# A new hand-written order of the 1,380 steps of a fused attention and mixture kernel on one core

## The chip, the cores and the metric

One core of one Trainium2 chip. The metric is device microseconds of one execution; lower is better. The time shown for a kernel is the median of several runs.

## What is computed

Eight batches of 512 tokens in 8 heads of 64, and 32 state rows a head. Both directions of a small cross attention are made, and their results go side by side through one wide layer with a "snake" activation:

```python
scores = scale * x @ state.T ;  a  = softmax(scores)  ;  xread = a @ state     # 512 rows a batch
scores2 = scale * state @ x.T;  a2 = softmax(scores2) ;  sread = a2 @ x        # 32 rows a batch
x = concat([xread, sread])            # 8 * 544 = 4352 rows of 512
h = x @ w_in                          # 512 -> 2048
g = h + sin(alpha * h)**2 / (alpha + 1e-9)
out = g @ w_out                       # 2048 -> 512
```

## The kernel before, in words

There is no loop. A list of names, `ORDER`, is written out by hand, and the kernel walks through it and calls one small function for each name. Each engine has a queue of its own and works through its instructions in the order in which the list issued them; the framework puts in the waits that the data and the buffers need. So the list fixes what stands ahead of what on TensorE (PE), VectorE (DVE), ScalarE (ACT), GpSimd (POOL) and the DMA queues of SyncE (SP) and POOL. Where a step's name ends in A, V or G it runs on ACT, DVE or POOL. A number after `t` below is the batch; "batch 8" is the 256 `sread` rows.

The steps, with the lines that the profile shows for them:

- `lq`, `l_s01` (SP queue, L261, L249), `l_st`, `li.s`, `lo.s`, `lx.b` (POOL queue, L267, L282, L294, L275): loads. `li.s` is the s-th quarter of w_in, `lo.s` the s-th quarter of w_out, 512 KB each as they arrive; `lx.b` is x of batch b. DMA steps of POOL stand in the same queue as its arithmetic.
- `warm_up.n.c.bank` (L303): n matmuls on zeros with c columns, whose result nobody reads.
- `st_t`, `st_c` (L333, L340): transpose of the state and copies out of PSUM; `xtq`, `xt`, `xc`, `at`, `ac` the same for x of batches 0 and 1 and for the weights of batch 0.
- `sc` (L399) scores, `ex` (L406) exponential, `rs`, `rr` (L410, L416) row sums and reciprocals, `nm` (L201, "A<-E,rR") normalising on POOL, `ad` (L440) a DMA transpose of the result for batches 1 to 7.
- `pk`, `td` (L348, L389): x of a batch repacked by DVE and transposed by DMA on the SP queue, which `sc` of that batch needs.
- `m.b.s` and `me` (L488, L496): state times a quarter (or two) of w_in, and its copies out of PSUM. h of the `xread` rows is then made from `m` directly, with the softmax weights as the moving operand. `m` uses the PE array in pieces of 64x32.
- `w`, `cs`, `rc`, `xs` (L450, L461, L468, L471): the `sread` side; `cs` uses the array in pieces of 128x64.
- `hg`, `h.t.f` (L552, L537, L543): h of batch t for the f-th 128 of 2048 columns; `si` (L560) sine, `sq` (L569 on ACT, L201 on DVE or POOL) its square, `gt` (L576) g.
- `o.t.st.f0.f1` (L587): out of 128 rows, from g of blocks f0 to f1-1; `oc`, `os` (L595, L602) copy and store.

Each matmul step names its PSUM bank (0 to 7); a bank can be written again only when the reader of its last content is through (for an `h`, that is its `gt`). The last sixteen matmuls, `oh.7.3.1`, fill a quarter of the columns of one row block.

```python
for step in ORDER:
    name, *args = step.split(".")
    getattr(steps, name)(*(int(a) if a.isdigit() else a for a in args))
```

Of the kernel before, what the change touches and what calls it, by code (L numbers as in the profile page):

```python
# [33 lines left out]
warm_up.2.128.2 gt.0.2 si.0.0 warm_up.2.128.2 warm_up.2.128.6 warm_up.2.128.3 warm_up.2.128.2
warm_up.2.128.6 me.0.1.0.A gt.0.1 sq.0.0.G m.0.2.3.2 si.0.3 m.1.2.5.6 hg.0.4.0.7 me.0.2.0.V
me.0.2.1.A hg.0.4.1 sq.0.3.G hg.0.6.0.4 me.1.2.1.V hg.0.6.1 si.0.4 hg.0.7.0.3 hg.0.11.0.2 me.1.2.0.V
si.0.6 hg.0.7.1 sq.0.4.G hg.0.5.0.6 gt.0.0 hg.0.5.1 si.0.7 hg.0.11.1 hg.0.8.0.5 hg.0.8.1 sq.0.6.A
gt.0.3 sq.0.7.G o.0.3.0.2.0 si.0.5 gt.0.4 o.0.3.2.3 o.0.0.0.2.1 si.0.11 o.0.0.2.3 gt.0.6 sq.0.5.G
o.0.0.3.4 o.0.2.0.1.7 si.0.8 o.0.3.3.5 sq.0.11.A gt.0.7 hg.0.9.0.4 sq.0.8.G o.0.2.1.2 gt.0.5
o.0.2.2.4 hg.0.9.1 gt.0.11 o.0.0.4.5 hg.0.10.0.3 si.0.9 o.0.2.4.5 gt.0.8 o.0.0.5.6 o.0.3.5.6  # L40
sq.0.9.A o.0.3.6.8 pk.1.0.V hg.0.10.1 xt.1.1.6 pk.1.1.V si.0.10 gt.0.9 xt.1.0.2 xc.1.1.0.A sq.0.10.G
o.0.2.5.6 xc.1.1.1.V xc.1.0.0.A o.0.0.6.7 xc.1.0.1.V o.0.0.7.8 o.0.2.6.7 sc.1.1.5 gt.0.10 sc.1.0.4
m.0.3.6.2 ex.1.0 o.0.2.7.8 me.0.3.0.V o.0.1.0.3.3 me.0.3.1.V o.0.1.3.6 hg.0.13.0.6 o.0.1.6.7 ex.1.1
rs.1.0 hg.0.13.1 m.1.3.2.4 si.0.13 o.0.1.7.8 rr.1.0 rs.1.1 nm.1.0.0.4.G o.0.1.8.9 hg.0.12.0.5
o.0.3.8.9 rr.1.1 hg.0.12.1 me.1.3.0.V o.0.0.8.9 nm.1.1.0.4.G o.0.1.9.10 o.0.0.9.10 me.1.3.1.V
si.0.12 o.0.0.10.11 o.0.3.9.11 sq.0.13.G ad.1 hg.0.15.0.2 sq.0.12.A o.0.1.10.12 hg.0.15.1 gt.0.12
o.0.2.8.10 si.0.15 o.0.2.10.11 gt.0.13 o.0.0.11.12 hg.0.14.0.4 sq.0.15.A hg.0.14.1 o.0.3.11.13
si.0.14 gt.0.15 o.0.0.12.13 o.0.1.12.13 o.0.3.13.14 sq.0.14.A pk.2.0.V o.0.1.13.14 pk.2.1.V h.1.2.5
gt.0.14 h.1.4.6 td.2 si.1.2 lx.3.0.1 h.1.0.2 si.1.4 o.0.0.13.15 sq.1.2.V h.1.1.4 si.1.0 gt.1.2
sq.1.4.G o.0.3.14.16 si.1.1 o.0.2.11.13 sq.1.0.A oc.0.3.V h.1.6.5 sq.1.1.G gt.1.4 o.0.2.13.14 os.0.3  # L50
h.1.3.0 si.1.6 gt.1.0 o.0.1.14.16 si.1.3 sq.1.6.G h.1.13.6 gt.1.1 oc.0.1.A o.0.2.14.15 o.0.0.15.16
si.1.13 h.1.15.2 sq.1.3.G gt.1.6 os.0.1 o.0.2.15.16 oc.0.0.A h.1.5.4 sq.1.13.G oc.0.2.V si.1.15
h.1.7.3 os.0.0 gt.1.3 o.1.1.0.1.5 si.1.5 os.0.2 h.1.8.1 sq.1.15.G gt.1.13 o.1.1.1.2 si.1.7
o.1.2.0.2.7 sq.1.5.A o.1.1.2.3 sq.1.7.G h.1.12.0 gt.1.15 si.1.8 h.1.9.6 gt.1.5 o.1.2.2.3 si.1.12
sq.1.8.G o.1.2.3.5 gt.1.7 si.1.9 o.1.1.3.4 h.1.10.2 sq.1.12.A pk.3.1.V h.1.11.4 sq.1.9.G gt.1.8
o.1.2.5.6 si.1.10 o.1.2.6.7 gt.1.12 h.1.14.3 si.1.11 sq.1.10.G o.1.2.7.8 gt.1.9 sc.2.1.1 si.1.14
o.1.1.4.7 sq.1.11.A pk.3.0.V sq.1.14.G o.1.1.7.8 gt.1.10 td.3 o.1.2.8.9 sc.2.0.0 o.1.1.8.9 gt.1.11
o.1.1.9.10 ex.2.0 o.1.3.0.2.6 gt.1.14 o.1.3.2.4 o.1.2.9.10 o.1.3.4.5 o.1.2.10.12 ex.2.1 o.1.2.12.13
rs.2.0 o.1.1.10.11 m.2.2.2.4.3.0 rr.2.0 rs.2.1 o.1.2.13.14 nm.2.0.0.4.G me.2.3.0.A o.1.2.14.15 w.0.1
rr.2.1 me.2.2.1.A me.2.3.1.V o.1.3.5.6 nm.2.1.0.4.G me.2.2.0.A o.1.3.6.7 o.1.2.15.16 cs.0 oc.1.2.A  # L60
m.2.0.3.4.0.2 ad.2 rc.0 o.1.3.7.8 me.2.1.1.A o.1.3.8.9 sc.3.0.7 xs.0.1 me.2.1.0.A o.1.1.11.12 os.1.2
me.2.0.0.V sc.3.1.2 me.2.0.1.A o.1.1.12.13 o.1.3.9.10 xs.0.0 o.1.3.10.11 ex.3.0 o.1.1.13.16 ex.3.1
rs.3.0 o.1.3.11.13 oc.1.1.A o.1.3.13.14 rr.3.0 h.2.0.0 rs.3.1 nm.3.0.0.4.G os.1.1 o.1.3.14.16 si.2.0
rr.3.1 h.2.1.3 oc.1.3.V nm.3.1.0.4.G h.2.2.4 h.2.8.1 os.1.3 h.2.3.7 lx.4.0.1 ad.3 si.2.2 o.1.0.0.3.2
si.2.8 sq.2.0.V o.1.0.3.4 sq.2.2.G gt.2.0 h.2.4.5 si.2.1 o.1.0.4.6 si.2.3 sq.2.8.G o.1.0.6.7 gt.2.2
h.2.9.6 si.2.4 o.2.3.0.1.0 o.1.0.7.8 sq.2.1.G o.1.0.8.9 sq.2.3.A gt.2.8 o.1.0.9.10 h.2.5.4 si.2.9
gt.2.3 o.1.0.10.11 sq.2.4.G o.1.0.11.12 si.2.5 h.2.7.1 gt.2.1 o.1.0.12.13 sq.2.9.A sq.2.5.G
o.1.0.13.14 gt.2.4 o.1.0.14.15 si.2.7 o.1.0.15.16 o.2.0.0.1.7 gt.2.9 o.2.0.1.2 oc.1.0.A h.2.6.3
sq.2.7.G gt.2.5 o.2.3.1.2 os.1.0 o.2.3.2.3 si.2.6 h.2.10.5 pk.4.1.V pk.4.0.V o.2.3.3.4 sq.2.6.A
# [594 lines left out]
```

## Time and profile before

| | |
|---|---|
| median of 7 runs | 221.22 us (221.15 to 221.54) |
| the profiled execution | 221.41 us, of which the span is 219.5 |
| TensorE clock granted | 1.00 |
| PE busy | 210.0 us (96%), 1593 matmul records |
| DVE, ACT, POOL busy | 162.2 (74%), 173.4 (79%), 107.0 (49%) |
| o (L587), h (L537) | 133.9 and 60.0 us busy |
| loads of w_in, w_out, x | 512 KB each, 10.9, 17.6, 7.5 us from issue to landing (medians) |

The span runs from the first to the last instruction; the 1.9 us around it are start and end of the program. A row of the timeline has the start, the time until the last of its instructions ended, the engine, the line and how many instructions it merges; idle time ahead of it and what ended that stand in brackets. Matmuls overlap: a matmul of 512 columns is shown with 0.38 us, but in a dense row one starts every 0.216 us.

### The profile page before, as it was taken

Reading aid. Unit: us, or ns where it says so; the run is one execution under the profiler, and the core shown is the slowest. Engines: PE = TensorE matmul, PEld = TensorE weight load, DVE = VectorE, ACT = ScalarE, POOL = GpSimd, SP = SyncE. Lnnn points to the kernel's source line nnn. Section 1 sums busy time; section 2 is a strip of 40 time slices with the busy share of each in tenths; the row PEclk is TensorE's granted clock in tenths of the full one; section 3 lists DMA queues with packets and bytes.
Section 4 is the critical chain, followed back from the end, with each engine's and each line's share of the span. In section 5 each row is a group of like instructions: output and inputs, shape, how many; then the busy total and the mean of one; then the engine's idle time right before and its main releaser. Section 6 shows DMA issues by size and latency. Waiting matters only on the chain.

```text
span 219.5 us, 4304 instructions
## 1 busy us (share of the span) xinstructions
PE 210.0 (96%) x1593; PEld 104.5 (48%) x1619; DVE 162.2 (74%) x286; ACT 173.4 (79%) x297; POOL 107.0 (49%) x115
## 2 busy tenths in 40 slices
PE   6789999999999999999999999999999999999994
PEld 3644544444444534444454444444444555665452
DVE  2769896999668889989888788888667987671201
ACT  4699878997899979898996999798858896685111
POOL 5959534795296647743943387273501082121000
PEclk9999999999999999999999999999999999999999
DMA  6999999935378529167135327470220211012042
GB/s 184 194 207 204 205 204 124 212 128 96 99 159 129 99 78 154 51 152 92 51 72 127 114 77 96 130 114 0 48 100 0 99 48 48 0 51 96 1 143 96
DMA packets 38052, 23.48 MB, mean 107 GB/s; under 512 B 20992, under 2 KB 33680, under 8 KB 38032
## 3 DMA queue, kind: packets, MB, share of 16 engines
q1 hardware_dynamic: 26128, 15.08, 26.2%
q0 software_dynamic: 11648, 8.13, 26.0%
q8 instruction: 12, 0.20, 0.4%
q14 instruction: 8, 0.07, 0.1%
q10 hardware_dynamic: 256, 0.01, 0.1%
HBM read 17.44 MB, written 8.91 MB: 120 GB/s over the span
## 4 chain that ended last, share of the span: by engine, by line
PE 86%; DMA 4%; ACT 3%; DVE 2%; POOL 2%; issue 1%
PE o_ps L587 51%; PE h_ps L537 20%; PE m_ps L488 4%; PE h_ps L543 3%; DMA st_nat<-in_state_dram 3%; PE h_ps L552 3%; DVE gT L576 2%; PE w_ps L450 2%; POOL s L201 2%; PE s_ps L399 1%; PE w_ps L461 1%; DMA s<-in_state_dram 1%; ACT s L560 1%; PE warm_ps L303 1%; ACT L226 1%
## 5 line engine op out<-in xcount | busy, mean ns | idle before, releaser
L587 PE MATMUL o_ps<-w_out_sb,gT 128*128 128x512 bf16 (+2 forms) x542 | 133.9, 373 | 1.6 <-issue 1.0
L576 DVE SCALAR_TENSOR_TENSOR gT<-s,inva_sb,h_ps 128x512 bf16<-128x512 bf16 (+1 forms) x144 | 96.6, 714 | 18.9 <-POOL s L201 9.7
L201 POOL TENSOR_TENSOR s<-s 128x512 bf16<-128x512 bf16 (+1 forms) x76 | 76.6, 1019 | 63.8 <-ACT s L560 61.7
L560 ACT ACTIVATE s<-h_ps,alpha_sb 128x512 bf16<-128x512 f32 (+1 forms) x144 | 88.7, 670 | 10.6 <-PE h_ps L543 4.5
L587 PEld LDWEIGHTS <-gT 128*128 128x128 bf16 x560 | 52.4, 98 | 60.3 <-issue 5.0
L537 PE MATMUL h_ps<-AT,M 128*128 128x512 bf16 x219 | 60.0, 379 | 0.3
L537 PEld LDWEIGHTS <-M 128*128 128x128 bf16 x224 | 21.8, 98 | 25.9 <-issue 0.4
L569 ACT ACTIVATE s<-s 128x512 bf16<-128x512 bf16 (+1 forms) x53 | 31.4, 594 | 0.8
L201 POOL TENSOR_TENSOR A<-E,rR 128x512 bf16<-128x512 bf16 x16 | 16.6, 1048 | 23.8 <-ACT o_sb L595 12.7
L595 ACT COPY o_sb<-o_ps 128x512 f32<-128x512 f32 (+2 forms) x24 | 13.7, 570 | 16.6 <-PE o_ps L587 16.5
L496 ACT CAST M<-m_ps 128x512 bf16<-128x512 f32 x35 | 18.6, 594 | 8.2 <-PE m_ps L488 8.2
L496 DVE CAST M<-m_ps 128x512 bf16<-128x512 f32 x29 | 18.9, 679 | 2.4 <-PE m_ps L488 2.1
L595 DVE COPY o_sb<-o_ps 128x512 f32<-128x512 f32 x11 | 7.6, 690 | 13.0 <-PE o_ps L587 12.9
L410 DVE TENSOR_REDUCE R<-E 128x16 f32<-128x512 bf16 x16 | 10.4, 658 | 1.2 <-ACT E L406 0.9
L201 DVE TENSOR_TENSOR s<-s 128x512 bf16<-128x512 bf16 (+1 forms) x15 | 6.2, 415 | 6.8 <-ACT s L560 6.7
L488 PE MATMUL m_ps<-w_in_sb,stT 64*32 64x512 bf16 x256 | 10.2, 382 | 0.0
L468 DVE RECIPROCAL rC<-w_ps 128x128 f32<-128x128 f32 x8 | 7.6, 948 | 3.3 <-PE w_ps L461 3.2
L552 PE MATMUL h_ps<-AT,M 128*128 128x512 bf16 x29 | 8.4, 379 | 1.0 <-ACT M L496 0.8
L303 PE MATMUL warm_ps<-warm 128*128 128x128 bf16 (+1 forms) x66 | 7.1, 260 | 2.2 <-DVE warm L209 2.0
L406 ACT ACTIVATE E<-s_ps 128x512 bf16<-128x512 f32 x16 | 8.9, 603 | 0.4 <-PE s_ps L399 0.3
L543 PE MATMUL h_ps<-xs_all,w_in_sb 128*128 128x256 bf16 x64 | 9.1, 273 | 0.0
L560 ACT ACT_TABLE_LOAD x5 | 6.4, 1283 | 2.2 <-PE h_ps L537 1.1
(56 smaller groups left out, 100.9 us busy)
## 6 DMA issues: line engine op xcount, KB each, us to landing
out_dram<-o_sb SPq DMA_DIRECT2D x33, 256.0 KB, 2.3
xnat<-in_x_dram POOLq DMA_DIRECT2D x7, 512.0 KB, 7.5
w_in_sb<-in_moe_w_in_dram POOLq DMA_DIRECT2D x4, 512.0 KB, 10.9
w_out_sb<-in_moe_w_out_dram POOLq DMA_DIRECT2D x4, 512.0 KB, 17.6
x<-in_x_dram SPq DMA_DIRECT2D x4, 256.0 KB, 4.1
st_nat<-in_state_dram POOLq DMA_DIRECT2D x1, 256.0 KB, 5.9
out_dram<-o_sb SPq DMA_DIRECT2D x1, 192.0 KB, 1.9
s<-in_state_dram SPq DMA_DIRECT2D x1, 128.0 KB, 2.3
```

Of the source, the lines that this page charges most:

```text
L201: {"V": k.nc.vector, "G": k.nc.gpsimd}[eng].tensor_tensor(out, a, b, ALU.mult)
L410: k.nc.vector.reduce_sum(R[:, g], k.t["E", b][:, g].rearrange("p c (h j) -> p (c h) j", j=k.Ns), axis=AX.X)
L488: k.nc.tensor.matmul(k.t["m", b, s + n, g][o0:o0 + k.Ns, :], k.stT[k.half(r), b * k.G + g, c0:c0 + k.Ns], k.w_in_sb[k.half(r), 2 * g + h, ...
L496: k.copy(eng)(k.t["M", b][:, g, s * k.FW:(s + 1) * k.FW], k.t["m", b, s, g][:])
L537: k.nc.tensor.matmul(hp[:, :n], k.t["M", t][:, g, fs], k.t["AT", t][:, g, :], start=(g == 0), stop=(g == k.G - 1),)
L543: k.nc.tensor.matmul(hp[:, :n], k.w_in_sb[:, q, fs], k.xs_all[:, q].rearrange("p b j -> p (b j)"), start=(q == 0), stop=(q == k.Q - 1),)
L552: k.nc.tensor.matmul(k.t["h", t, f][:], k.t["M", t][:, g, f * k.P:(f + 1) * k.P], k.t["AT", t][:, g, :], start=(g == 0), stop=(g == k.G - 1),)
L560: k.nc.scalar.activation(s[:, :n], k.t["h", t, f][:, :n], ACT.Sin, scale=k.alpha_sb[:, f:f + 1])
L569: k.nc.scalar.activation(s2[:, :n], s[:, :n], ACT.Square)
L576: k.nc.vector.scalar_tensor_tensor(gT[:, :n], k.t["s2", t, f][:, :n], k.inva_sb[:, f:f + 1], k.t["h", t, f][:, :n], ALU.mult, ALU.add,)
L587: k.nc.tensor.matmul(k.t["o", t, st, half][:, cols], k.t["gT", t, f][:, rows], k.w_out_sb[:, f, cols], start=(f == 0), stop=(f == k.FT - 1),)
L595: k.copy(eng)(o_sb[:, cols], k.t["o", t, st, half][:, cols])
```

## The change

Only `ORDER` changes: 1380 names become 1371. The steps that compute are the same (the matmuls in `o` are cut into 378 names and not 388), on the same lines; what differs is their order on the engines, the PSUM banks, and the engine of a few copies and squares: `sq` on ACT 53 to 48 and on POOL 76 to 81, `me` on ACT 35 to 36, `oc` on ACT 22 to 21, `st_c` on ACT 3 to 2, one `nm` from POOL to DVE. The warm-up matmuls go from 60 of 128 columns and 6 of 512 to 67 and 7. On POOL's queue `lx.1` and `lo.1` change places; `lo.0` stands behind `li.2` and ahead of `li.3` in both lists. The final steps stay the same, but `oc.7.2` moves from DVE to ACT.

The diff replaces the whole list. Its first part, and the stretches that the prediction speaks of:

```diff
-touch_x l_s01 zero.1 touch lq.0.S ident_ consts warm_up.2.128.0 warm_up.2.128.1 warm_up.2.128.2
-l_alpha lq.1.S zero.0 warm_up.6.512.3 exp_table lq.2.S identf.V lq.3.S s01_c.G l_st li.0 xq.0.A
-s01_t.4 li.1 xtq.0.5 xq.1.A s01_k.1.V s01_k.0.A li.2 xtq.1.6 xc.0.0.0.V xq.2.A xc.0.0.1.V lo.0
-al_t.7 xq.3.A xtq.2.0 al_c inva sc.0.0.1 lo.1 xc.0.1.0.A xtq.3.2 warm_up.2.128.3 ex.0.0
-warm_up.2.128.4 lx.1.0.1 warm_up.2.128.5 xc.0.1.1.V warm_up.2.128.6 warm_up.2.128.7 rs.0.0 sc.0.1.0
-li.3 st_t.0.3 ex.0.1 rr.0.0 st_t.1.4 lo.2 st_c.0.0.V st_c.0.1.A warm_up.2.128.5 warm_up.2.128.6
-warm_up.2.128.1 st_c.1.0.A rs.0.1 warm_up.2.128.2 warm_up.2.128.7 nm.0.0.0.4.G warm_up.2.128.0
-warm_up.2.128.5 st_c.1.1.A warm_up.2.128.3 warm_up.2.128.6 warm_up.2.128.1 rr.0.1 warm_up.2.128.2
-sin_table warm_up.2.128.7 warm_up.2.128.0 nm.0.1.0.4.G at.0.0.5 warm_up.2.128.3 ac.0.0.V m.0.0.6.4
...
-m.2.0.3.4.0.2 ad.2 rc.0 o.1.3.7.8 me.2.1.1.A o.1.3.8.9 sc.3.0.7 xs.0.1 me.2.1.0.A o.1.1.11.12 os.1.2
...
+touch_x l_s01 consts touch lq.0.S ident_ l_alpha lq.1.S zero.0 warm_up.7.512.3 exp_table lq.2.S
+zero.1 identf.V lq.3.S s01_c.G l_st li.0 xq.0.A xtq.0.4 warm_up.3.128.3 li.1 xq.1.A s01_t.5
+xc.0.0.0.V li.2 xtq.1.6 warm_up.5.128.3 xq.2.A s01_k.1.V lo.0 al_t.7 s01_k.0.A xc.0.0.1.V xtq.2.0
+warm_up.3.128.3 xq.3.A al_c sc.0.0.1 inva lx.1.0.1 xc.0.1.0.A xtq.3.2 warm_up.2.128.3
+warm_up.2.128.4 ex.0.0 lo.1 warm_up.2.128.5 xc.0.1.1.V warm_up.2.128.6 warm_up.2.128.7 sc.0.1.0
+rs.0.0 st_t.1.3 li.3 ex.0.1 st_t.0.4 rr.0.0 lo.2 st_c.1.1.A st_c.1.0.V warm_up.2.128.5
+warm_up.2.128.6 sin_table warm_up.2.128.2 rs.0.1 warm_up.2.128.7 warm_up.2.128.1 nm.0.0.0.4.G
+warm_up.2.128.0 warm_up.2.128.5 warm_up.2.128.3 warm_up.2.128.6 warm_up.2.128.2 rr.0.1
+warm_up.2.128.7 warm_up.2.128.1 st_c.0.0.V warm_up.2.128.0 warm_up.2.128.5 nm.0.1.0.4.G st_c.0.1.A
+at.0.0.3 warm_up.2.128.6 ac.0.0.V m.0.0.2.7 m.1.0.1.0 lo.3 at.0.1.5 me.0.0.1.A me.0.0.0.V
+warm_up.2.128.6 warm_up.2.128.4 me.1.0.1.A ac.0.1.V hg.0.2.0.3 me.1.0.0.V hg.0.0.0.7 hg.0.2.1
+hg.0.0.1 hg.0.3.0.6 si.0.2 lx.2.0.1 hg.0.3.1 m.1.1.2.4 si.0.0 m.0.1.5.0 hg.0.1.0.1 me.0.1.1.A
+sq.0.2.V hg.0.1.1 sq.0.0.G me.1.1.0.V me.1.1.1.A warm_up.2.128.0 gt.0.2 si.0.3 warm_up.2.128.0
+warm_up.2.128.2 warm_up.2.128.4 warm_up.2.128.0 warm_up.2.128.2 me.0.1.0.A gt.0.0 sq.0.3.G m.1.2.4.0
+si.0.1 m.0.2.3.2 hg.0.4.0.5 me.1.2.1.V me.0.2.0.A hg.0.4.1 sq.0.1.G hg.0.5.0.7 me.0.2.1.V hg.0.5.1
+si.0.4 hg.0.8.0.0 hg.0.10.0.3 me.1.2.0.V si.0.5 hg.0.10.1 sq.0.4.G hg.0.8.1 gt.0.1 hg.0.7.0.2
+si.0.10 o.0.2.0.1.4 hg.0.7.1 gt.0.3 si.0.8 sq.0.5.G o.0.2.1.3 hg.0.6.0.1 sq.0.10.A gt.0.4 o.0.2.3.4
...
+me.1.3.1.A o.0.0.14.15 o.0.3.13.14 pk.2.1.V me.1.3.0.A o.0.3.14.15 pk.2.0.V o.0.1.13.14 o.0.3.15.16
+o.0.1.14.15 td.2 h.1.2.2 oc.0.3.V h.1.1.1 si.1.2 lx.3.0.1 h.1.3.3 si.1.1 h.1.0.0 os.0.3 sq.1.2.V
...
+sc.2.0.0 si.1.5 gt.1.3 h.1.13.4 sq.1.4.G o.1.1.0.1.7 si.1.6 gt.1.14 o.1.1.1.2 h.1.8.3 sq.1.5.A
...
+me.2.0.1.V o.1.0.0.2.4 me.2.1.0.A o.1.2.9.10 me.2.0.0.V os.1.1 w.0.7 cs.0 sc.3.1.1 rc.0 sc.3.0.3
...
+gt.2.5 si.2.4 o.1.0.14.15 h.2.11.2 si.2.9 gt.2.2 h.2.10.1 sq.2.4.G o.1.0.15.16 si.2.11 gt.2.0
+h.2.7.6 sq.2.9.A sq.2.11.G gt.2.4 h.2.6.3 o.2.0.0.1.5 oc.1.0.A o.2.0.1.2 gt.2.9 o.2.0.2.3 si.2.6
+h.2.15.7 os.1.0 pk.4.1.V o.2.3.0.1.4 si.2.7 o.2.3.1.2 sq.2.6.G gt.2.11 o.2.3.2.4 si.2.10 o.2.3.4.6
+sq.2.7.A pk.4.0.V h.2.12.0 sq.2.10.G gt.2.6 td.4 h.2.13.2 si.2.15 gt.2.7 o.2.0.3.5 si.2.13 sq.2.15.G
...
```

Where the eight `cs` stand: before, `cs.0`, `cs.2`, `cs.3` and `cs.6` have an `m` right behind them, `cs.7` and `cs.5` stand together, `cs.1` and `cs.4` alone between full-array steps. After, `cs.2` has an `m` behind it and `cs.1` one ahead of it, `cs.7` and `cs.5` stand together, and `cs.0`, `cs.3`, `cs.4` and `cs.6` have neither.

## The prediction

> **What bounds the kernel now.** I read the page first, for the engine that is full, then the chain that ended last, the waits of PE, and the timeline of the stages where PE waits.
>
> ```profile
> PE 210.0 (96%) x1593; PEld 104.5 (48%) x1619; DVE 162.2 (74%) x286; ACT 173.4 (79%) x297; POOL 107.0 (49%) x115
> ...
> PE 86%; DMA 4%; ACT 3%; DVE 2%; POOL 2%; issue 1%
> ```
>
> PE is the bound, but 96% hides where its other time is. From the chain, piece by piece, and PE's own waits:
>
> ```profile
> 202.14 6.26 PE o_ps L587 x29
> ```
>
> ```profile
> PE x_ps L361 <- ACT xp L356: 1.0, 2, 0.8
> PE o_ps L587 <- issue: 1.0, 6, 0.2
> ```
>
> 29 matmuls in 6.26 us are 0.216 us each. PE waits only microseconds in all, and apart from the "issue" entry, which is mostly a matmul without a record behind an `m`, all of it is early. From 18.5 us to the end, I added 0.216 for each 512-column matmul, 0.109 for 256 columns, 0.029 for each of `sc` and `w`, and the blocks priced below: the sum follows the trace within 0.1 us to the last matmul. So after 18.5 us PE has nothing left to lose. An order can gain only before that, and lose anywhere.
>
> **Before 18.5 us.** These rows are ACT's chain:
>
> ```profile
> 10.59 1.45 ACT L340 COPY stT<-st_ps 64x384 bf16<-64x384 bf16 x3 [0.94 <-DVE stT L340]
> 12.06 1.28 ACT L226 ACT_TABLE_LOAD   x1
> ...
> 13.58 1.07 ACT L496 CAST M<-m_ps 128x512 bf16<-128x512 f32 x2
> 14.85 1.26 ACT L560 ACTIVATE s<-h_ps,alpha_sb 128x512 bf16<-128x512 f32 x2 [0.19 <-PE h_ps L552]
> ...
> 17.62 0.60 ACT L496 CAST M<-m_ps 128x512 bf16<-128x512 f32 x1
> ```
>
> The last copy ends at 18.22 and lets go the steady stage at 18.27. The loads set floors: the state lands at 9.28, the first three quarters of w_in at 11.8, 15.2 and 17.1 (issue times 4.16, 4.90 and 5.63, plus 7.7, 10.3 and 11.5 to landing). POOL's first ten issues are the same but for one swap, so these stay.
>
> The new list gives ACT one `st_c` less ahead of the sine table, so table and first copies of M come some 0.5 us earlier. Something else takes that wait's place. The bracket of the first row shows that the two engines' copies of one transposed block go one after the other, in the list's order; the new list puts ACT's first. DVE's `st_c.1.0.V` then starts at about 10.5 (10.0 + 0.47) instead of 10.0, and behind it in DVE's queue stand `rs.0.1`, `rr.0.1`, and then POOL's `nm.0.1`:
>
> ```profile
> 10.00 0.55 DVE L340 COPY stT<-st_ps 64x384 bf16<-64x384 bf16 x1 [0.26 <-PE st_ps L333]
> ...
> 11.58 1.05 POOL L201 TENSOR_TENSOR A<-E,rR 128x512 bf16<-128x512 bf16 x1 [0.19 <-DVE rR L416]
> ```
>
> So `nm.0.1` runs 12.1 to 13.15, `at.0.1` goes at 13.3, `ac.0.1` 13.75 to 14.2, and `hg.0.2.1` at 14.2, where it is now (14.22, behind ACT's copy). From there both lists hold the same chain with other block numbers: four `hg`, two `m`, six warm-ups, ACT's six instructions. **Nothing gained**; bounds -0.2 (the 0.5 comes through, until the quarter landing at 15.2 stops it) and +0.1. The seven added warm-up matmuls and the earlier `consts` lie in waits for loads; the two before `at.0.0` (2 x 0.056 = 0.11) end before `nm.0.1` does. Without that cover they cost 0.11.
>
> `lx.1` ahead of `lo.1`: each landing is about 2.6 us behind the one before (19.7, 22.2, 24.9 by the tiles' answers). x of batch 1 comes at 22.4 and is first used (`xt.1.1`) at 23.3; the second quarter of w_out comes at 24.9 and is first used (`o.0.0.4.5`) at 25.4, both placed by counting 0.216s from 18.27. Cost nothing, hidden by 0.9 and 0.5 us of matmuls; without that cover, the lateness itself.
>
> **Blocks in pieces of the array.** Here the new list costs something certain. `cs` alone, and `cs` with `m` behind it:
>
> ```profile
> 150.87 1.03 PE L537 MATMUL h_ps<-AT,M 128*128 128x512 bf16 x4
> 151.83 0.41 PE L461 MATMUL w_ps<-E,ones 128*64 128x128 bf16 x8
> 152.18 1.25 PE L587 MATMUL o_ps<-w_out_sb,gT 128*128 128x512 bf16 x5
> ```
>
> ```profile
> 163.85 0.63 PE L450 MATMUL w_ps<-E,xp 128*128 128x64 bf16 x16
> 164.41 0.41 PE L461 MATMUL w_ps<-E,ones 128*64 128x128 bf16 x8
> 164.76 0.62 PE L488 MATMUL m_ps<-w_in_sb,stT 64*32 64x512 bf16 x16
> 165.54 0.81 PE L587 MATMUL o_ps<-w_out_sb,gT 128*128 128x512 bf16 x3 [0.16 <-issue]
> ```
>
> Alone: 150.87 + 4 x 0.216 = 151.73 to 152.18 is 0.45. An `m` of 16 alone (78.19 to 78.85 in PE's timeline) is 0.66. Together: 163.85 + 16 x 0.029 = 164.31 to 165.32 (a matmul without a record stands 0.216 ahead of the last row) is 1.01, so neighbours save 0.10. Before, four pairs; after, two. **+0.20**, on PE's full path. Bounds 0 (a `cs` beside `sc`, which the trace doesn't show, might save the same) and 0.46 (two whole borders of 0.23).
>
> [...]
>
> **New waits after 18.5.** (1) `o.0.2.1.3` needs `gt.0.1`:
>
> ```profile
> 17.82 6.57 POOL L201 TENSOR_TENSOR s<-s 128x512 bf16<-128x512 bf16 x6 [0.36 <-ACT s L560]
> ...
> 19.97 5.37 DVE L576 SCALAR_TENSOR_TENSOR gT<-s,inva_sb,h_ps 128x512 bf16<-128x512 bf16 x8
> 20.76 1.95 PEld L587 LDWEIGHTS <-gT 128*128 128x128 bf16 x10 [0.21 <-DVE gT L576]
> ```
>
> Its square is POOL's second of these six, 18.92 to 19.97; `gt` 20.05 to 20.79; the matmul at 20.95. By count it is due at 20.67: eleven matmuls stand before it now, where twelve stood. **+0.25**, bounds 0 and 0.3. The squares that move from ACT to POOL cost 1.04 in place of 0.64 us; the tightest places that I found between 41 and 53 us come out within 0.1 of their due time, at 0.
>
> (2) `sc.2.0.0` stood 12 us of PE work behind `td.2`; now 5.8.
>
> ```profile
> 34.28 0.94 POOL L275 DMA_DIRECT2D xnat<-in_x_dram  x1
> ...
> 37.90 3.19 SPq L389 DMA_TRANSPOSE xT<-xp  x1
> ```
>
> `td.2` stays near 37.95 (behind `gt.0.15` and both `pk.2` on DVE). `lx.3` goes behind one more square of POOL, to about 36.1, and so runs beside `td.2`. Such a transpose lands after 4.3 us alone (`td.3`), 5.4 in this place now; `ad.4`, issued 0.1 us after `lx.5`, took 6.7 where `ad.2` took 3.0. `sc.2.0.0` is due at 44.0 by the count with (1) in it, 6.05 behind the issue. Bounds: 0 (5.4) and 4.3 + 3.7 - 6.05 = 2.0. The nearest row is `td.2` itself, but its neighbour comes 1.8 us later now: I take **+0.2**. PE is in order, so everything waits behind it.
>
> [...]
>
> (3) DVE waits at `pk.4.1` for x of batch 4 (0.9 us now, hidden); that load goes some 0.3 us later, and one more `gt` stands ahead of `gt.2.6`, which `o.2.3.6` needs. Bounds 0 and 0.3, **+0.05**.
>
> (4) Between 26 and 29 us, where `sc.1`, `m.0.3` stand in one lump now, the count loses 0.1; spread out it should not: **-0.1** (bounds -0.1 and 0). The end: `oc.7.2` on ACT (0.59) ends before the last sixteen matmuls do (0.87 us long): 0, bounds -0.05 and +0.1.
>
> **Sum:** 0 + 0.20 + 0.25 + 0.2 + 0.05 - 0.1 = +0.6 on the profiled execution, 221.41, so 222.0; that execution stood 0.19 above the median of 221.22, so as a median **221.8 us**.
>
> **The rivals.**
>
> - *Not slower (0.36).* The transpose is in time, and the early copy frees 0.2: if DVE's `st_c.1.0.V` doesn't wait for ACT's, `rs.0.1` starts before 10.7 and `hg.0.2.1` goes by 14.0. Then -0.2 + 0.20 + 0.25 - 0.1 = +0.15: 221.4. It decides below 221.66. Against it: the 0.94 in the bracket above. An order that only shuffles hidden work, so doesn't do what its words say (`lo.0` is ahead of `li.3` in both lists), falls in here too, at +0.2.
> - *Transpose very late (0.12).* `lx.3` holds `td.2` as `lx.5` held `ad.4`: 2.0 in place of 0.2, so 223.6; half of that gives 222.7. It decides once `td.2` takes over 7 us.
> - *Faster by over 0.2% (0.07).* Under 220.78. It needs the early -0.2, no term (1) and `cs` without a price: -0.3, and a little that I don't see.
> - *The forecast (0.45):* 221.66 to 222.4.
>
> 0.2% is 0.44 us, about what a measurement can tell from no change. Slower 0.45 + 0.12 = 0.57, same 0.36, faster 0.07. Range: the early gain with the pairs' price gives 221.2, and a bit of the faster case is taken in: 221.05; above, half of the late transpose and an unseen stall: 222.9.
>
> **What would show it.** Right: the steady stage starts within 0.15 us of 18.27; `cs.0`, `cs.3`, `cs.6` with 0.45 each; a gap of PE ahead of `o.0.2.1`; `td.2` to landing over 6 us and PE idle at `sc.2.0.0`. Wrong: `hg.0.2.1` by 13.8, or PE gaps in places that I priced at nothing, between 40 and 110 us above all.

## The result, and the profile after

The changed kernel takes **226.66 us** (median of 12 runs, 223.28 to 228.53) where the kernel before takes 221.24 (median of 31, 220.93 to 222.85). The ratio is 1.0152, 95% interval 1.0124 to 1.018; it leaves out the six runs in which the mean clock fell to 0.990 to 0.992, as described below, and the profiled execution is one of these six. That execution took 227.37 us (span 225.3), 5.96 more than the one of before.

The lines of the page that answer to those of the prediction, with the granted clock, after:

```profile
PE 214.1 (95%) x1601; PEld 105.2 (47%) x1627; DVE 164.5 (73%) x288; ACT 170.9 (76%) x291; POOL 110.0 (49%) x119
...
PEclk9999999979999999999999999999999999999999
...
PE 70%; DMA 11%; issue 5%; POOL 5%; DVE 4%; ACT 3%; POOLq 0%
```

And the clock before:

```profile
PEclk9999999999999999999999999999999999999999
```

PE is still full on the average. What is new is a 7 in the ninth slice of the clock (45 to 51 us), and DMA with 11% of the chain in place of 4%. PE's own waits name the place (time in all, times, longest):

```profile
PE s_ps L399 <- DMA xT<-xp: 2.9, 1, 2.9
...
PE h_ps L537 <- DVE gT L576: 0.2, 1, 0.2
```

One wait of 2.9 us, at `sc.2.0.0` for `td.2`. The timelines of POOL and SP, against the two rows of before:

```profile
36.26 0.94 POOL L275 DMA_DIRECT2D xnat<-in_x_dram  x1
38.09 6.02 SPq L389 DMA_TRANSPOSE xT<-xp  x1
```

`lx.3` goes 2 us later than before, `td.2` 0.2 later. `td.2` holds SP's queue for 6.02 us in place of 3.19 and lands at 46.76, after 8.7 us in place of 5.4. Then the windows of PE (busy, matmuls, granted clock, DMA share, GB/s):

```profile
40.00:43.90 3.90, 3.85 (x18) 1.00 1.45 115
43.90:46.70 2.80, 0.04 (x1) 1.00 1.20 237
...
47.90:51.30 3.40, 3.40 (x9) 0.50 0.50 136
51.30:55.00 3.70, 3.65 (x24) 1.00 0.00 0
```

PE does nothing from 43.9 to 46.7. Soon after, from 47.89 to 51.31, the granted clock is 0.5 and a matmul of 512 columns starts every 0.427 us, not every 0.216.

Counting each matmul at its price, as for the prediction, and comparing with the trace gives the account of the profiled execution: steady stage at 18.20 in place of 18.27 (-0.07); `hg.0.8.0`, an early `h` that waits for a copy of ACT, +0.2; `sc.2.0.0` +3.0; half clock +1.7; `h.4.8` near 102 us +0.4; `cs` without neighbours +0.2; the last store lands 3.2 us behind the last copy in place of 2.8, +0.4. The sum is 5.8, the difference of the spans. That is one execution; those of 223.3 can't have had all of it. A second profiled execution of the same kernel (e16 below, 224.46 us) lost 1.35 at `sc.2.0.0`, 0.7 in the opening, and had no half clock.

### The profile page after: what moved, and what is told of

It reads as the page before. It is cut to its first block, busy times and chain, and to the rows that moved or that the text cites. A ratio compares the mean times of both kernels' runs of the same rounds, so it can differ in the third digit from the quotient of the medians.

```text
span 225.3 us, 4314 instructions
## 1 busy us (share of the span) xinstructions
PE 214.1 (95%) x1601; PEld 105.2 (47%) x1627; DVE 164.5 (73%) x288; ACT 170.9 (76%) x291; POOL 110.0 (49%) x119
## 4 chain that ended last, share of the span: by engine, by line
PE 70%; DMA 11%; issue 5%; POOL 5%; DVE 4%; ACT 3%; POOLq 0%
PE o_ps L587 42%; PE h_ps L537 14%; DMA xT<-xp 4%; DMA xnat<-in_x_dram 4%; PE h_ps L543 3%; DVE gT L576 3%; DMA st_nat<-in_state_dram 3%; PE h_ps L552 3%; PE m_ps L488 3%; POOL s L201 2%; POOL A L201 2%; PE w_ps L450 2%; ACT s L560 1%; PE s_ps L399 1%; PE w_ps L461 1%
## 5 line engine op out<-in xcount | busy, mean ns | idle before, releaser
L587 PE MATMUL o_ps<-w_out_sb,gT 128*128 128x512 bf16 (+2 forms) x542 | 132.2, 374 | 1.5 <-issue 0.6
L201 POOL TENSOR_TENSOR s<-s 128x512 bf16<-128x512 bf16 (+1 forms) x81 | 80.8, 1013 | 69.8 <-ACT s L560 64.2
L569 ACT ACTIVATE s<-s 128x512 bf16<-128x512 bf16 (+1 forms) x48 | 28.8, 606 | 0.6
L201 POOL TENSOR_TENSOR A<-E,rR 128x512 bf16<-128x512 bf16 x15 | 15.5, 1048 | 24.4 <-DVE rR L416 9.0
L496 ACT CAST M<-m_ps 128x512 bf16<-128x512 f32 x36 | 19.4, 591 | 9.7 <-PE m_ps L488 9.6
L595 ACT COPY o_sb<-o_ps 128x512 f32<-128x512 f32 (+2 forms) x23 | 13.1, 569 | 17.2 <-PE o_ps L587 17.1
L496 DVE CAST M<-m_ps 128x512 bf16<-128x512 f32 x28 | 18.3, 683 | 5.1 <-PE m_ps L488 5.0
L595 DVE COPY o_sb<-o_ps 128x512 f32<-128x512 f32 x12 | 8.3, 688 | 8.9 <-PE o_ps L587 8.9
L488 PE MATMUL m_ps<-w_in_sb,stT 64*32 64x512 bf16 x256 | 10.2, 382 | 0.0
L303 PE MATMUL warm_ps<-warm 128*128 128x128 bf16 (+1 forms) x74 | 8.8, 266 | 1.4 <-DVE warm L209 1.2
L399 PE MATMUL s_ps<-stT,xT 128*128 128x64 bf16 x128 | 5.9, 193 | 2.9 <-DMA xT<-xp 2.9
```

The costliest lines, as they stand in the source:

```text
L201: {"V": k.nc.vector, "G": k.nc.gpsimd}[eng].tensor_tensor(out, a, b, ALU.mult)
L488: k.nc.tensor.matmul(k.t["m", b, s + n, g][o0:o0 + k.Ns, :], k.stT[k.half(r), b * k.G + g, c0:c0 + k.Ns], k.w_in_sb[k.half(r), 2 * g + h, ...
L496: k.copy(eng)(k.t["M", b][:, g, s * k.FW:(s + 1) * k.FW], k.t["m", b, s, g][:])
L569: k.nc.scalar.activation(s2[:, :n], s[:, :n], ACT.Square)
L587: k.nc.tensor.matmul(k.t["o", t, st, half][:, cols], k.t["gT", t, f][:, rows], k.w_out_sb[:, f, cols], start=(f == 0), stop=(f == k.FT - 1),)
L595: k.copy(eng)(o_sb[:, cols], k.t["o", t, st, half][:, cols])
```

## The experiments

All kernels compute the whole result. Each is set beside runs of the kernel before on its own chip (medians 221.27 to 221.44).

### The transpose beside the load

e1 and e2 move `lx.3` forward on POOL, e3 moves only PE's score back, e4 fills PE's wait.

```diff
 e1: -... sq.0.13.G ... sq.0.15.G ... lx.3.0.1    +... lx.3.0.1 sq.0.13.G ... sq.0.15.G
 e2: -... sq.0.15.G ... lx.3.0.1                  +... lx.3.0.1 sq.0.15.G
 e3: -... sc.2.0.0 ... (6 us of PE work) sc.2.1.2 +... sc.2.0.0 sc.2.1.2
 e4: -... sc.2.0.0                                +... warm_up.13.512.0 sc.2.0.0
```

> The changed kernel with lx.3 two squares of POOL earlier (issued at about 33.4 us in place of 36.26, ahead of sq.0.13 and sq.0.15). Theory (the transpose td.2 can't end before lx.3 has passed, then the idle PE gets half the clock): lx.3 lands by 41.5, td.2 issued at 38.0 lands at 43 to 44, so after 4.3 to 5.5 us; PE waits less than 0.3 us at sc.2.0.0 and there is no stretch of half clock: 221.9 to 222.6. Rival A (squares on POOL and the DVE chain between 40 and 53 us are too slow): lx.3 earlier delays sq.0.13, the loss stays, 225 to 227. Rival B (the early score is late whatever loads): td.2 still takes over 7 us, 226 to 227.

> The changed kernel with lx.3 one square earlier (issued at about 35.2). Theory: the landing of td.2 moves with that of lx.3, which is 1.1 earlier, so td.2 lands at about 45.6 after 7.6 us, PE waits about 1.8 at sc.2.0.0; a wait that short may leave the clock whole: 223.0 to 225.0, between the kernel after and the run with two squares. [...] Rival A: 225 to 227.

> The changed kernel with only PE's sc.2.0.0 moved 6 us of PE work back, to right ahead of sc.2.1; no DMA and no POOL step moves. Theory: td.2 still takes 8 to 9 us (lands near 46.7), but nobody waits for it: no wait of PE for xT, no half clock, 221.9 to 222.6. Rival A (POOL's squares, DVE's chain): PE waits over 1.5 us for gT or s between 43 and 53, 224 to 227.

> The changed kernel with 13 warm-up matmuls of 512 columns (2.8 us) ahead of sc.2.0.0, so that PE works through the wait. Theory: td.2 lands as late as before (8.7 us) and sc.2.0.0 starts at the same time near 46.7, but PE was not idle and its clock stays whole: the 3 us stay, the 1.7 us of half clock go: 224.4 to 225.4. Rival C (the slow matmuls after the wait come from late operands, not from the clock): 226 to 227.5, with PE at 0.427 us a matmul after 47.9 as in the kernel after.

Measured: e1 224.53 us, e2 224.39, e3 223.97, e4 227.11. None came down to 222, for a reason that was on no list: in all four profiles the steady stage starts at 19.5 to 20.3 us, 1.3 to 2 later than in the profile of after, in front of every edit. That is taken up in the next part. Behind that delay the mechanism shows. With the score late (e3) `td.2` took 9.2 us and nobody waited for it; e6 below differs from e5 by this move alone and is 1.33 us faster. With the load earlier (e1, e2) `td.2` took 5.3 us and the score waited 0.2 us at most. But in e1 the load met another transpose, `ad.1`, issued 0.08 us behind it, which took 7.2 us in place of 3.3:

```profile
PE h_ps L537 <- DMA AT<-A: 2.3, 1, 2.3
```

So rival A falls (nothing waits for squares there), rival B falls, and my numbers for e1 and e2 fall with the unseen loss. In e4 the fill ended 1.2 us after the landing, so it cost more than it could save.

One run takes the load out of the way altogether, together with the longer warm-up of the next part:

```diff
 e7: -td.2 ... lx.3.0.1 ... sc.2.0.0 ... sq.1.4.G    +td.2 ... sc.2.0.0 ... sq.1.4.G lx.3.0.1
     -warm_up.7.512.3                                +warm_up.10.512.3
```

> The changed kernel with 10 opening warm-ups and with lx.3 behind the first square that follows sc.2.0.0 on POOL, so that td.2 has no load beside it; the score stays early. Theory: td.2 lands 4.3 us after its issue, ahead of sc.2.0.0, no wait of PE there; lx.3 is issued near 45 us and lands near 51, ahead of its first use: 222.0 to 222.6. Rival (td.2 is slow in this place whatever runs beside it): over 7 us again, 224 to 226.5.

`td.2` landed after 4.9 us and no wait stood at `sc.2.0.0`. The time was 225.31 all the same: PE waited 1.4 us at two `o` for `gT`, behind the squares among which `lx.3`'s issue now stands on POOL, and x of batch 1 landed 1.1 us later in this run (0.8). The transpose is cured, the kernel isn't.

Over all profiles one number held. `td.2` landed 1.67 to 2.52 us behind the landing of `lx.3` in every one of the 19 in which that load was in flight, whether it was issued 1.8 or 4.9 us behind the load's issue, while its own time went from 5.3 to 9.2 us. Before: 41.60 and 43.29. After: 44.33 and 46.76.

### The opening and the clock

What is 1.3 to 2 us late in e1 to e4 is PE's clock. The first record of full clock in the trace starts at 4.64 us before, at 6.93 after, and at 10.2 to 12.0 in e1 to e4. Ahead of it the traces have no clock record (a table of windows shows 1.00 there), but the matmuls run at half the pace: in the traces of before and after the warm-ups of 512 columns start every 0.427 us, not every 0.216. PE's warm-ups before, and the opening matmuls of after (start, length until the last ended):

```profile
2.00 3.08 PE L303 MATMUL warm_ps<-warm 128*128 128x128 bf16 x12 [2.00 <-DVE warm L209]
```

```profile
1.19 3.17 PE L303 MATMUL warm_ps<-warm 128*128 128x512 bf16 x7 [1.19 <-DVE warm L209]
4.75 0.61 PE L361 MATMUL x_ps<-ident,xp 128*128 128x128 bf16 x4 [0.39 <-ACT xp L356]
...
7.29 0.40 PE L361 MATMUL x_ps<-ident,xp 128*128 128x128 bf16 x4
```

The warm-ups start at 1.19 (before: 2.00) and end at 4.36 (before: 5.08); then PE idles until x has landed. The same seven warm-ups with a gap of 0.39 us behind them go with full clock at 6.93 (after), 0.55 with 9.52 (e16), and 0.72 to 1.10 with 10.2 to 12.0 (e1 to e4). The transposes take 0.61 us until the clock is full, 0.40 from then on. e5 makes the warm-ups longer, e6 adds the late score, and e8 puts the gap into the kernel before:

```diff
 e5: -warm_up.7.512.3    +warm_up.10.512.3
 e6: e5 and e3
 e8: -warm_up.6.512.3 ... xq.0.A s01_t.4 ... xtq.0.5
     +warm_up.4.512.3 ... xq.0.A ... xtq.0.5 s01_t.4
```

> The changed kernel with 10 opening warm-up matmuls of 512 columns in place of 7, nothing else. Theory (two separate losses: the opening warm-ups end at 4.4 us and leave PE idle until the first x lands, so that the full clock comes at 7 to 12 us in place of 4.6; and td.2 late at sc.2.0.0): full clock by 5.5 us, the steady stage at 18.1 to 18.4 us in place of 18.2 to 20.3; the second loss stays, 223.2 to 226.5, less spread between executions than before the edit. Rival (the early spread comes from the loads' landings, not from the clock): steady stage still at 19 to 20.3 us though the clock is full early.

> Both edits together: 10 opening warm-ups and sc.2.0.0 right ahead of sc.2.1. Theory: both losses go; what remains is 0.2 of cs without neighbours, 0.2 of o.0.2.1, 0.4 near 102 us and 0.2 of small ones: 222.0 to 222.5. Rival (a third loss, not seen yet): over 223.

> The kernel before with 4 opening warm-ups of 512 columns in place of 6, and xtq.0 ahead of s01_t as in the changed kernel, so that PE idles at 4.4 us until x has landed. Theory: the full clock comes at 7 to 12 us in place of 4.64, the steady stage 0.2 to 2 us later than 18.27, differing between executions: 221.5 to 223.3. Rival (the early loss of the changed kernel comes from the order of ACT's and DVE's copies): within 0.3 us of the kernel before.

e5: 224.59 us (224.49 to 225.38), steady stage at 18.19. e6: 223.26, at 17.97. e8: **222.87 us**, 1.55 over its neighbours, ratio 1.0068 (1.0051 to 1.0086), steady stage at 19.97. PE's opening in e8, and then in e6:

```profile
2.00 2.53 PE L303 MATMUL warm_ps<-warm 128*128 128x128 bf16 x10 [2.00 <-DVE warm L209]
5.09 0.61 PE L361 MATMUL x_ps<-ident,xp 128*128 128x128 bf16 x4 [0.56 <-ACT xp L356]
...
10.03 0.64 PE L399 MATMUL s_ps<-stT,xT 128*128 128x64 bf16 x8
```

```profile
1.19 4.45 PE L303 MATMUL warm_ps<-warm 128*128 128x512 bf16 x10 [1.19 <-DVE warm L209]
5.43 0.64 PE L361 MATMUL x_ps<-ident,xp 128*128 128x128 bf16 x4
...
6.66 0.40 PE L361 MATMUL x_ps<-ident,xp 128*128 128x128 bf16 x4
```

With the gap of 0.56 us, and one of 0.69 at 7.7 us, the pace is half until 12.68 us in e8; without a gap at 4.4 the clock is full at 6.29 in e6 (in the opening of before: 4.64, and 6.15 and 6.26 in e17 and e15). e8 has less warm-up as well as the gaps, so by itself it doesn't part the two; after, e16 and e1 to e4, with equal warm-ups, do. This is a second loss of the change, up to 2 us at the start of the steady stage in some executions and little in others, and it may explain part of the spread from 223 to 228. In the total it is worth less: e6 differs from e3 by the longer warm-up alone, its profile starts the steady stage 2.3 us sooner, and its time is only 0.71 us shorter, since PE then loses 0.9 us near 73 us, where e3 loses nothing (the third loss). With both losses out, e6 still lies 2 us over before, more than I expected. Of that, 1.3 us are the third loss, below (0.9 near 73 us, 0.4 near 98).

### The half clock behind the wait

e11 and e13 were to lengthen PE's idle time by moving `sc.2.0.0` forward (by 0.9 and 1.7 us of PE work; in e13 and e14 `gt.1.0`, which frees its bank, goes with it), e12 and e14 fill it, and e16 is the changed kernel once more. All but e16 have the longer opening.

```diff
 e11: -h.1.5.1 ... h.1.6.5 os.0.2 sc.2.0.0   +sc.2.0.0 h.1.5.1 ... h.1.6.5 os.0.2
 e12: e11 with warm_up.8.512.0 ahead of sc.2.0.0
 e13: -oc.0.1.V o.0.2.14.15 ... sc.2.0.0     +oc.0.1.V gt.1.0 sc.2.0.0 o.0.2.14.15 ...
 e14: e13 with warm_up.9.512.0 ahead of sc.2.0.0
```

> The changed kernel with 10 opening warm-ups and with sc.2.0.0 0.9 us of PE work earlier, ahead of h.1.5, so that PE idles about 2.8 us there in place of the 1.96 of the run with warm-ups alone (224.59). The end of the wait is the same, and the two h that stood ahead come behind it. Theory of the clock (an idle stretch near 3 us halves the clock for 3.4 us): the profile shows half clock near 46 to 52 us in some executions, mean clock 0.990 to 0.993 there, 226.0 to 227.0; executions without it 224.5 to 225.2. Rival (the half clock of the changed kernel had another cause): clock 0.997 or more in all executions, 224.4 to 225.2.

> The same with 8 warm-up matmuls of 512 columns (1.7 us) ahead of sc.2.0.0. Theory of the clock: PE idles about 1.1 us, the clock stays at 0.997 or more in all executions, 224.4 to 225.3, faster than the run without the fill by about 1.5 us. Rival: the same time as without the fill, within 0.3 us.

> The changed kernel with 10 opening warm-ups and with sc.2.0.0 1.7 us of PE work earlier (ahead of o.0.2.14), so that PE idles some 3.0 to 3.7 us until td.2 lands. Theory of the clock (an idle stretch near 3 us or longer halves the clock for 3.4 us; 2.1 and 2.3 us did not): half clock near 46 to 52 us in most executions, mean clock 0.990 to 0.993, 225.8 to 227.0, that is 1.3 to 1.9 over the 224.5 of the runs with a shorter idle stretch. Rival (the half clock of the changed kernel has nothing to do with the length of that wait): clock 0.997 or more, 224.2 to 225.2.

> The same with 9 warm-up matmuls of 512 columns (1.9 us) ahead of sc.2.0.0, which PE would otherwise idle away. Theory of the clock: idle 1.1 to 1.8 us, clock 0.997 or more in all executions, 224.2 to 225.2. Rival: as without the fill, within 0.3 us.

> The changed kernel once more, beside the others on one chip. Theory of the clock and of the opening: executions with mean clock 0.990 to 0.993 at 226.5 to 228.5, and others at 223.3 to 225.6; in the profile, a late full clock (7 to 12 us) or a half clock near 48 us, or both, where the time is over 225. Rival: all executions within 0.5 us of each other.

e11: 224.45 us, and PE was idle for only 1.77 us at the score, since `td.2` landed sooner (44.27); clock 0.997 or more in all runs, so it tests nothing, and e12 (225.31) had no half clock to remove. e13: 227.03 us, two of four runs at a mean clock of 0.992 (227.74 and 227.54), the others at 1.000 (225.42 and 226.52). Its wait, and its windows of PE:

```profile
44.74 0.41 PE L399 MATMUL s_ps<-stT,xT 128*128 128x64 bf16 x8 [2.55 <-DMA xT<-xp]
...
41.80:44.70 2.90, 0.39 (x2) 1.00 1.16 227
45.00:48.40 3.40, 3.40 (x14) 0.50 0.69 210
48.50:52.00 3.50, 3.50 (x18) 1.00 0.00 0
```

PE is idle for 2.55 us at the score, then 3.41 us run at half clock, which costs 1.7: the picture of after, with the opening mended. In e14 the clock is 0.997 or more in all four runs; its time, 226.20, isn't what I expected, because the fill ran 0.8 us past the landing. e16: 224.46 to 229.23, three of six at 0.985 to 0.992, the control that was wanted; but one run of 227.82 kept 1.000, so the clock isn't the whole of the spread.

So the half clock followed the long wait here, and not in every execution. Idle stretches of 2.86 us (after) and 2.55 (e13) brought it in the profiles; 2.33, 1.77 and 1.60 (e1, e11, e5) did not. With the long wait in place the mean clock fell in 11 of 22 runs (after, e16, e13), with the shorter one of e5 and e11 in none of eight; where it is filled, moved or gone (e1 to e4, e6, e7, e9, e12, e14) it is 0.997 or more in all 36. The wait isn't shown to be the only source: one run of e10 and one of e17 have 0.992 too, and behind the opening their profiled executions show no idle stretch over 1.45 and 0.25 us.

The clock records show the lengths. The half clock lasted 3.413 us in the trace of after (from 47.89) and 3.41 in e13; the idle stretch ahead of it was shorter both times, 2.86 and 2.55 us. The full clock lasted 215.04 us before (63 times 3.413), and after 40.96 (12 times) ahead of the half clock and 174.08 (51 times) behind it; in all 19 profiles that record both, the time from the first full clock to the next change was such a multiple (12, or 61 to 64). Counted in stretches of that length, PE was idle for 2.32 us (after) and 2.55 (e13) in the last one ahead of the half clock; the most in any other between opening and end was 1.77 (e11), and e1's 2.33 fell into two, 1.46 and 0.87. Two stretches at half clock are too few to show what decides.

### A third loss: DVE's copies beside POOL's squares

In e6, PE loses 0.9 us to waits for `gT` near 73 us, where after and e3 lose nothing. The rows of POOL and DVE there, for e6 and then for e3:

```profile
70.44 3.39 POOL L201 TENSOR_TENSOR s<-s 128x512 bf16<-128x512 bf16 x3 [0.53 <-ACT s L560]
...
70.56 1.20 DVE L348 COPY xp<-xnat 128x1024 bf16<-128x1024 bf16 x1 [0.21 <-DMA xnat<-in_x_dram]
```

```profile
72.73 4.53 POOL L201 TENSOR_TENSOR s<-s 128x512 bf16<-128x512 bf16 x4 [0.54 <-ACT s L560]
...
72.68 0.43 DVE L348 COPY xp<-xnat 128x1024 bf16<-128x1024 bf16 x1
```

The same copy (`pk.4.1`) takes 0.43 us where it starts 0.05 ahead of POOL's square, and 1.20 where it starts 0.12 behind it. POOL's first square in e6 ends at 71.47, the copy at 71.76. Where a `pk` started 0.05 us or more behind the start of a running square, it ended 0.28 to 0.29 us after that square (after: 53.39 and 53.68, 100.78 and 101.07; before: 111.56 and 111.84), or after its usual 0.42 us where that was later. Before, x of batch 4 landed at 70.14 and no square ran then. What holds the copy up isn't shown by these rows, only when it starts and ends.

e9 puts three copies behind the `gt` that followed them, in e6:

```diff
-pk.4.1.V ... pk.4.0.V ... gt.2.6 td.4    +gt.2.6 pk.4.1.V pk.4.0.V td.4
-pk.5.0.V ... gt.3.9 ... gt.3.7           +gt.3.9 ... gt.3.7 pk.5.0.V
```

> The changed kernel with 10 opening warm-ups, sc.2.0.0 ahead of sc.2.1, and now DVE's pk.4.1, pk.4.0 and pk.5.0 behind the gt that stood right behind them (gt.2.6, gt.3.7). Theory (third loss: a copy of x on DVE that starts at the landing, while a square of POOL runs, ends only 0.28 us after that square, 1.2 in place of 0.43 us, and the gt behind it are late at o.2.0.3 and at h.4.8): PE's waits near 73 (0.9) and 98 (0.4) go; what is left is 0.2 of cs, 0.2 of o.0.2.1, 0.3 between 44 and 50, less the 0.3 that the early stage gained: 221.6 to 222.2. Rival (the waits only move, to the transposes td.4 and td.5 and the scores behind them): 222.6 to 223.5.

224.56 us, the rival's way and worse. The waits near 73 and 98 went (0.8 us at another `o`, at 75, came), and `td.4`, issued later, brought back about as much as they had cost:

```profile
PE s_ps L399 <- DMA xT<-xp: 1.2, 1, 1.2
```

(x of batch 1 landed late in this run too, 0.7 us.) Who makes the copy late makes the transpose late. So the third loss is read from these rows; no run shows it by taking it out.

### The early part alone

Four kernels take over parts of the changed opening into the kernel before; e15 and e17 differ in the banks of `st_t`.

```diff
 e10: the first 97 names of after (with warm_up.10.512.3, hg.0.2.0 in bank 5), then before from hg.0.1.0.4 on
 e15: -st_t.0.3 ex.0.1 rr.0.0 st_t.1.4 lo.2 st_c.0.0.V st_c.0.1.A ... st_c.1.0.A ... st_c.1.1.A ... sin_table
      +st_t.1.3 ex.0.1 rr.0.0 st_t.0.4 lo.2 st_c.1.1.A st_c.1.0.V ... sin_table ... st_c.0.0.V ... st_c.0.1.A
 e17: e15 with st_t.1.4 and st_t.0.3
 e18: -l_s01 zero.1 ... consts warm_up.2.128.0 warm_up.2.128.1 warm_up.2.128.2 ... zero.0 warm_up.6.512.3
      +l_s01 consts ... zero.0 zero.1 warm_up.9.512.3
```

> The early part alone: the changed kernel's first 97 names (to the first h of batch 0, with 10 opening warm-ups) and then the list of before. Theory (the sine table off ACT's path to the first copies of M is worth 0.3 us, everything that is lost comes later): steady stage at 17.9 to 18.05 us with the state's landing at 9.3, and the rest as before: 220.8 to 221.1, ratio 0.998 to 0.9995. Rival (the gain needs the changed blocks behind it): 221.2 to 221.6.

> The kernel before with only its state section in the changed kernel's order: st_t.1 first, then ACT's st_c.1.1, DVE's st_c.1.0, the sine table, and st_c.0.0 and st_c.0.1 behind nm.0.1; banks, loads, warm-ups and all behind at.0.0 as before. Theory (the sine table off ACT's path to the copies of M is worth 0.3 us in the early stage, and nothing behind it needs the changed blocks): steady stage 0.2 to 0.35 us sooner against the state's landing, 220.8 to 221.15, ratio 0.998 to 0.9998. Rival (a start sooner by 0.3 us moves DMAs of later batches beside each other, as in the run with the early part alone): 221.4 to 223.

> The kernel before with its state section in the changed kernel's order as in the run with the table sooner, but with st_t.0 in bank 3 and st_t.1 in bank 4, so that m.0.0, which is written to banks 6 and 4, doesn't wait for ACT's st_c.0.1. Theory (the sine table off ACT's path is worth 0.3 us there): from the first st_t to the steady stage 8.6 to 8.7 us in place of 8.95, 220.8 to 221.15, ratio 0.998 to 0.9998. Rival (the gain needs the changed order of hg as well): 8.85 to 9.0, ratio 0.9995 to 1.001.

> The kernel before with only its opening changed the other way: consts ahead, so that the warm-up matmuls start at 1.2 us in place of 2.0 and run as 9 of 512 columns to the same 5.0 us. Theory (where the warm-ups fill PE until x has landed, the full clock comes by 4.6 us or sooner in every execution, and the state's landing sets the rest): the same median, within 0.3 us of before, full clock at 3.5 to 5.5 us. Rival (warm-ups that start sooner put the clock's change elsewhere and cost time): 221.6 or more, full clock over 6 us.

e10: 226.53 us. It was badly made: `hg.0.2.0` in bank 5 waited for the copy of `at.0.1` out of that bank (0.45 us), and `lo.1` behind `lx.1` doesn't suit the blocks of before:

```profile
PE s_ps L400 <- DMA xT<-xp: 1.5, 1, 1.5
PE o_ps L588 <- DMA w_out_sb<-in_moe_w_out_dram: 1.2, 1, 1.2
...
PE h_ps L538 <- DMA AT<-A: 1.1, 1, 1.1
```

e15 put `st_t.0` into a bank that `m.0.0` needs, which cost what it should gain (221.53, ratio 1.001, 0.9982 to 1.0038). e17, with the banks mended, has the steady stage 8.84 us after the first `st_t`, where before has 8.95 and after, e6, e9 and e11 8.62 to 8.67: a third of the gain. 221.20 us against 221.41, ratio 0.9989 (0.9961 to 1.0016): not told from before. e18: 221.17 us, 0.9982 (0.9961 to 1.0004), 220.88 to 221.80 where before ran from 220.91 to 223.01 beside it. The earlier start of the warm-ups cost nothing that these runs show; its full clock came at 6.35 us, later than I expected. Whether e17 or e18 beats before isn't settled by these runs.

## Why the prediction was wrong, step by step

The forecast was 221.8 us with a range to 222.9; the run came 3.8 above that. **Term (2) failed**, the wait of `sc.2.0.0` for `td.2`, priced at +0.2 with bounds 0 and 2.0. It was 3.0 in the profile of after, 1.35 in e16, 1.8 and 1.9 in e5 and e11. The mechanism was named, and the rival "transpose very late" describes it with its point ("over 7 us"; it took 8.7), but it was sized at 2.0 and held to be unlikely. What failed is the choice of the nearest row: the transpose's own duration (5.4 us) was carried over, when what kept within 0.85 us over the 19 profiles is its distance to the load's landing (1.67 to 2.52). That stood in the profile before: 43.29 - 41.60 = 1.7. With it, the load's issue at 36.1 and its 7.3 us of before (34.28 to 41.60) give 43.4, and so 45.1, 1.1 us late at least; the load itself then took 8.1.

**The half clock was not in the sum at all**: 1.7 us in the profile of after, behind an idle stretch of 2.86. The wait itself had cost 3.0 there.

**"The seven added warm-up matmuls and the earlier `consts` lie in waits for loads"**, priced at 0, failed too: they do, but they end 0.7 us sooner than before, and behind the gap that follows the clock was full only at 6.93 to 12.0 us (after, e16, e1 to e4; 4.64 before). That cost 0 in the profile of after, 0.7 in e16, 1.3 to 2 in e1 to e4; 1.55 in e8.

**(a) The early copy: "nothing gained"**, bounds -0.2 and +0.1. The chain went much as worked out; these rows of ACT, DVE and POOL after answer to those of before:

```profile
10.76 1.28 ACT L226 ACT_TABLE_LOAD   x1
10.78 0.55 DVE L340 COPY stT<-st_ps 64x384 bf16<-64x384 bf16 x1 [0.86 <-ACT stT L340]
...
12.35 1.05 POOL L201 TENSOR_TENSOR A<-E,rR 128x512 bf16<-128x512 bf16 x1 [0.70 <-ACT tiny L226]
```

DVE does wait for ACT. Yet the steady stage comes 0.3 us sooner after the first `st_t` (8.62 against 8.95), just past my bound: the table comes 1.3 us earlier, and ACT's first copies of M come sooner. In e17, which takes over this section alone, a third of the gain appears; where the other two thirds come from stays open.

**(b) The lost pairs: +0.20** held. `cs.4` between two full-array rows:

```profile
150.73 0.38 PE L587 MATMUL o_ps<-w_out_sb,gT 128*128 128x512 bf16 x1
151.04 0.41 PE L461 MATMUL w_ps<-E,ones 128*64 128x128 bf16 x8
151.39 0.60 PE L537 MATMUL h_ps<-AT,M 128*128 128x512 bf16 x2
```

150.73 + 0.216 to 151.39 is 0.44. The 0.23 for a whole border, in the bounds, was my estimate; no row shows a border by itself.

**(1) `o.0.2.1`, +0.25**: 0.2 is lost close by, but not in that wait, so the size was luck. `gt.0.1` ended at 20.65, and `o.0.2.1` followed the matmul ahead of it (20.58) without a gap, at 20.79. What was late is `hg.0.8.0`, the first matmul that needs the third quarter of M. By count it was due at 19.08; ACT's copy ended at 19.22, and PE's weight load waited for it. Before, the first such matmul stood one place further back.

```profile
18.60 0.62 ACT L496 CAST M<-m_ps 128x512 bf16<-128x512 f32 x1
...
19.27 0.76 PEld L552 LDWEIGHTS <-M 128*128 128x128 bf16 x5 [0.52 <-ACT M L496]
```

**(3) `pk.4.1`, +0.05**, bounds 0 and 0.3: 0 in after, e3, e7, e11, e14 and e16, but 0.9 in e1, e2, e4, e5, e6, e12 and e13. The place was right, the bound not: the copy behind the landing was taken at its usual 0.43 us. **(4)** and the end, -0.1 and 0: the gain isn't there, and the last store landed 0.4 later.

**Places priced at nothing** "between 40 and 110 us above all": `h.4.8` near 102 us lost 0.4, since `lx.5`, issued 0.08 us ahead of `ad.4` as before, landed after 8.6 us (before: 7.5) and held `pk.5.0` and the `gt` behind it.

Of the 1.5 to 2.5%, then, the first cause is one score moved in front of a transpose that a load holds up; the second, which showed only in the runs, is an opening that lets PE idle. The order of the blocks itself cost the 0.2 that it was priced at.

## What to carry to other kernels

`td.2`, issued while a load of 512 KB was in flight, landed 1.67 to 2.52 us behind that load in 19 profiles, for own times from 5.3 to 9.2 us: to price a moved transpose or load, take the load's landing and add the distance of the two landings that the profile shows. Two idle stretches of PE, of 2.86 and 2.55 us (after, e13), had a second price of 1.7 us each, and gaps of 0.39 to 1.10 us in the opening went with a full clock at 6.93 to 12.0 us in place of 4.64; so count where a stretch of warm-up ends, not only how much of it there is. And a hand-made order that leaves 0.05 us between a copy and a square (0.43 us for the copy in e3, 1.20 in e6), or 0.1 between a load and a transpose (7.2 us for `ad.1` in e1, 3.3 in after), is several kernels in one: look at several profiles of it before believing one.

## What the runs showed of the hardware that was not expected

- `td.2` landed 1.67 to 2.52 us behind the load beside it in 19 profiles, for durations from 5.3 to 9.2 us; 4.9 us without a load (e7). In the trace of after, 491 packets of its queue start from 41.0 to 42.5 us, only 17 from 42.5 to 44.0, beside the load's last 34, and 412 in the half microsecond behind that.
- An `ad` issued 0.08 us behind a load took 7.2 us in place of 3.3 (`ad.1` in e1; 3.3 in after).
- Idle PE of 2.86 and 2.55 us was followed by 3.41 us of half clock (after, e13); 2.33, 1.77 and 1.60 us were not (e1, e11, e5). The full clock lasted whole multiples of 3.413 us in the 19 traces that record its end (40.96 us in after, 215.04 before).
- With gaps of 0.56 and 0.69 us behind 2.5 us of warm-up the full clock came at 12.68 us (e8; 4.64 to 6.26 in the profiles with the opening of before).
- DVE's copy of 128x1024 took 0.42 to 0.43 us alone and 1.20 (e6) beside a square of POOL that started 0.12 us ahead of it; where the square started 0.05 us or more ahead, the copy ended 0.28 to 0.29 us after it unless its own 0.42 us ended later.
